# Blocked attention and a gated feed-forward layer on one core: 2 KB pieces for the stored weight blocks, wider products of zeros, and a new placement of the steps

## The chip, the cores and the metric

The kernel runs on one core of a Trainium2 chip. The metric is the device time of one execution in microseconds (us). Three executions of the kernel before took 804.26, 806.49 and 806.54 us, a median of 806.49 us. The engines are PE (TensorE; its weight loads are PEld), DVE (VectorE), ACT (ScalarE), POOL (GpSimd) and SP (SyncE, which here only issues transfers). A transfer is issued in the program order of SP or of ACT (SPq and ACTq in the trace) and moved by 16 shared DMA engines.

## The reference

```
scores = (q @ k.T) / sqrt(64)               # 8 batches, 8 heads, 576 positions, head size 64
mask   = local (the last 32 keys)  for heads 0 to 3
         strided (every 32nd key)  for heads 4 to 7
attn   = softmax(where(mask, scores, -1e9)) ; x = attn @ v     # x: 4608 tokens x 512
h = x @ w_in                                # 512 x 2048
g = h if h >= 1;  0 if h <= -1;  else (h + 1)**2 / 4
out = g @ w_out                             # 2048 x 512
```

All inputs and the output are float32.

## The kernel before, in words

The masks leave only blocks of the score matrix, so each batch is four units of attention: u0 and u1 (local heads), u2 and u3 (strided heads). One unit goes through steps that the program names by a letter: scores on PE (`s`, L592), adding the mask while leaving PSUM (`m`, L652, DVE), row maximum (`x`, L678, DVE), subtracting it (`b` on DVE or `a` on POOL, L682), exponential (`e`, L689, ACT), row sum (`q`, L693, DVE), adding a small constant (`k` on DVE or `p` on ACT), reciprocal and normalising (`w` on DVE or `r` on POOL; L705, L706), a transpose on DVE (`t`, L743), a trip through DRAM (`j`, `J`), the product with v on PE (`v` or `V`, L779), and a split of the result into a high and a low part (`h` on ACT, L841, and `l` on DVE, L850). Two steps fetch q and k (`Q`) and v (`F`).

The feed-forward part makes each float32 product of three products of 128x512 in a reduced format (high by high, high by low, low by high). Tokens come in a chunk of 512 (c = 0), two more such chunks (c = 1 and 2), and then in blocks of 1024 tokens. For c = 0 to 2 the program loops over 16 slices f of the hidden size: 12 products (L887) make `h` for the slice, ACT bends and squares it (L891, L894), and DVE closes the slice with a gate (L897, the minimum of two values). The gate also frees the PSUM bank in which `h` was summed. For c = 1 and 2 the banks are b2 and b3 in turn for f = 0 to 3 of c = 1, and then b2, b3 and b0 in turn: so the products of f = 2 and 3 wait for the gates of f = 0 and 1, and from f = 5 on each slice waits for the gate of the slice three before it. For c = 0 and the last pieces of c = 0 inside c = 1, the products with w_out (L947) run between those of w_in.

From there on the kernel uses a scheme that needs seven products instead of eight for a two by two grid of blocks, and for it sums of weight blocks. These are made on the core: step `C` or `Y` adds the blocks (L499; on POOL or on DVE), `N` or `O` combines the sums (L504; POOL or DVE), `R` rounds them (L508, ACT), `D` keeps the rest (L512, DVE). `K` stores the weight blocks in DRAM (L490, L491) and `S` the sums (L515), both issued from ACT; `fetch_w` (L971) reads single blocks back on SP, into a ring of seven buffers. The blocks of 1024 tokens then run `up_block` (L1040) and `down_block` (L1135); for the latter `G.s` splits an operand on ACT and DVE (L996, L997), `G.t` (DVE) or `G.p` (POOL) makes a sum of operands (L1096), and `G.r` takes a result out of PSUM.

The order of all this is written out in the table AGENDA: a position in the PE program (in units of six products of 128x512, negative ones inside c = 0), and the steps that are emitted there. Nothing is moved afterwards: each engine runs its instructions in that order, and waits only for the data and the buffers that it needs. The first four lines of the table hold batch 0, with the raw loads and the splitting of the first weights, and 37 products of zeros (`Z`, L577), which write into PSUM banks that hold nothing yet.

Of the kernel before, what the change touches and what calls it, by code (L numbers as in the profile page):

```python
# [1326 lines left out]
```

## Time and profile before

| | before |
|---|---|
| runs, us | 804.26, 806.49, 806.54 (median 806.49) |
| the profiled execution: its own time, us | 806.21 |
| the profiled execution: span, first to last instruction, us | 804.4 |
| mean granted TensorE clock | 0.998 of 2.4 GHz |
| PE busy in the span | 793.8 us, 99% |
| DVE, ACT and POOL busy | 620.6, 505.2 and 258.2 us |

The span is what the profiler sees between the first and the last instruction of the program; the execution's own time is 1.8 us longer. PE is busy in nearly all of it, so the table alone says little: what can be won or lost is in the few places where PE waits, and in how close the engines that feed it run behind it. A row of the timeline gives the start, the duration, the engine, the line, the operation with the tile written and the tiles read, how many such instructions are merged in the row, and in brackets the idle time of the engine before it and what ended it.

### The profile page before, as it was taken

How to read it: one execution, taken by the hardware profiler on the slowest of the kernel's cores; microseconds unless marked ns; L12 is line 12 of the kernel's file. 1: busy time of each engine (PE TensorE's matmuls, PEld its weight loads, DVE VectorE, ACT ScalarE, POOL GpSimd, SP SyncE). 2: the span in 40 equal slices, each digit the busy share in tenths (PEclk: the TensorE clock that was granted, in tenths of full speed). 3: DMA queues.
4: the chain of work that ended last, by engine and by line, in shares of the span. 5: the costliest groups of instructions: out<-in, count | busy, mean ns of one | idle time of the engine just before them, and what ended most of it. 6: DMA issues, size and time to landing. Idle time of an engine off the chain costs nothing.

```text
span 804.4 us, 17840 instructions
## 1 busy us (share of the span) xinstructions
PE 793.8 (99%) x6921; PEld 648.5 (81%) x6921; DVE 620.6 (77%) x882; ACT 505.2 (63%) x857; POOL 258.2 (32%) x202
## 2 busy tenths in 40 slices
PE   8999999999999999999999999999999999999998
PEld 6778888788888877878888888888888888888886
DVE  5899879999898999978679787575777764566673
ACT  5899764566774555677764455778554667775442
POOL 5366335796674320022141102132434001224000
PEclk9999999999999999999999999999999999999999
DMA  9948878799899899898889778777777676666765
GB/s 348 407 187 273 319 271 324 254 290 307 282 322 319 292 295 352 272 295 275 256 247 292 239 222 266 261 233 211 223 248 239 210 238 198 192 194 189 217 200 170
DMA packets 107699, 209.78 MB, mean 261 GB/s; under 512 B 17760, under 2 KB 33376, under 8 KB 105568
## 3 DMA queue, kind: packets, MB, share of 16 engines
q1 hardware_dynamic: 100560, 179.15, 69.8%
q10 hardware_dynamic: 7056, 29.49, 9.5%
q8 instruction: 55, 0.90, 0.4%
q14 instruction: 28, 0.23, 0.1%
HBM read 161.94 MB, written 46.66 MB: 259 GB/s over the span
## 4 chain that ended last, share of the span: by engine, by line
PE 91%; DVE 5%; ACT 1%; DMA 1%; issue 1%; POOL 1%; SPq 0%; POOLq 0%; DVEq 0%
PE yo L1135 22%; PE y L1040 16%; PE h L887 13%; PE zo L1135 10%; PE z L1040 8%; PE xo L1135 5%; PE o L947 4%; PE x L1040 4%; PE xp L779 3%; PE sc L592 3%; DMA qk<-in_qk_s 1%; PE tp L719 1%; DVE st L512 1%; DVE pr L682 1%; DVE st L678 0%
## 5 line engine op out<-in xcount | busy, mean ns | idle before, releaser
L1135 PE MATMUL yo<-hl,wr 128*128 128x512 f32 x768 | 177.6, 390 | 0.0
L1135 PEld LDWEIGHTS yo<-hl,wr 128*128 128x128 f32 x768 | 143.6, 188 | 30.9 <-DVE hl L997 0.9
L1040 PE MATMUL y<-x,wr 128*128 128x512 f32 x576 | 139.9, 389 | 0.0
L1040 PEld LDWEIGHTS y<-x,wr 128*128 128x128 f32 x576 | 108.0, 188 | 22.5
L887 PE MATMUL h<-xq_a,w 128*128 128x512 f32 x384 | 123.5, 395 | 1.9 <-DVE g L897 1.9
L1096 POOL TENSOR_TENSOR ga<-gb,ga 128x1024 f32<-128x1024 f32 x17 | 44.1, 2598 | 235.9 <-DVE ga L897 175.6
L997 DVE TENSOR_TENSOR hl<-ga,hl 128x1024 fp32r<-128x1024 f32 x48 | 63.5, 1338 | 37.0 <-ACT hl L996 36.9
L1135 PE MATMUL zo<-hl,wr 128*128 128x512 f32 x384 | 89.5, 391 | 0.0
L887 PEld LDWEIGHTS h<-xq_a,w 128*128 128x128 f32 x384 | 72.0, 188 | 18.6 <-DVE g L897 2.8
L1135 PEld LDWEIGHTS zo<-hl,wr 128*128 128x128 f32 x384 | 71.5, 188 | 15.9 <-DVE hl L997 0.6
L996 ACT CAST hl<-ga 128x1024 fp32r<-128x1024 f32 x48 | 50.0, 1052 | 51.1 <-PE yo L1135 16.3
L887 PE MATMUL h<-xq_b,w 128*128 128x512 f32 x192 | 73.6, 391 | 0.1
L1040 PE MATMUL z<-x,wr 128*128 128x512 f32 x288 | 73.5, 391 | 0.0
L1040 PEld LDWEIGHTS z<-x,wr 128*128 128x128 f32 x288 | 53.7, 188 | 11.4 <-DVE ga L1022 0.2
L894 ACT ACTIVATE tmp<-tmp 128x512 f32<-128x512 f32 x96 | 60.8, 634 | 3.0
L997 DVE TENSOR_TENSOR hl<-gb,hl 128x1024 fp32r<-128x1024 f32 x36 | 48.7, 1366 | 14.4 <-ACT hl L996 14.3
L996 ACT CAST hl<-gb 128x1024 fp32r<-128x1024 f32 x36 | 37.7, 1056 | 31.3 <-PE zo L1135 15.3
L504 POOL TENSOR_TENSOR st<-st 128x256 f32<-128x256 f32 x48 | 50.5, 1054 | 14.2 <-DVE st L705 6.6
L897 DVE SCALAR_TENSOR_TENSOR ga<-ga,tmp 128x512 f32<-128x512 f32 x48 | 33.0, 688 | 28.3 <-ACT tmp L894 28.0
L891 ACT ACTIVATE u<-h,half 128x512 f32<-128x512 f32 x48 | 32.8, 684 | 31.4 <-PE h L887 23.9
L469 POOL TENSOR_TENSOR raw<-raw 128x512 uint32<-128x512 uint32 (+1 forms) x34 | 35.6, 1057 | 42.3 <-DVE raw L465 16.6
L682 POOL TENSOR_TENSOR pr<-pr,st 128x384 f32<-128x384 f32 (+3 forms) x17 | 25.6, 1508 | 67.8 <-DVE st L678 67.8
(124 smaller groups left out, 1413.1 us busy)
## 6 DMA issues: line engine op xcount, KB each, us to landing
wr<-ks SPq DMA_DIRECT2D x224, 256.0 KB, 4.0
wr<-kq SPq DMA_DIRECT2D x168, 256.0 KB, 3.4
ks<-st ACTq DMA_DIRECT2D x16, 1024.0 KB, 6.8
raw<-in_w SPq DMA_DIRECT2D x30, 512.0 KB, 9.6
qk<-in_qk_s SPq DMA_DIRECT2D x16, 604.0 KB, 6.4
qk<-in_qk_l SPq DMA_DIRECT2D x16, 576.0 KB, 6.4
kq<-w ACTq DMA_DIRECT2D x16, 512.0 KB, 3.6
v<-in_v_l SPq DMA_DIRECT2D x21, 384.0 KB, 5.2
```

Source lines behind the costliest of these rows:

```text
L469: nc.gpsimd.tensor_tensor(out=raw[:, :, 1], in0=raw[:, :, 1], in1=raw[:, :, 0], op=ALU.add)
L504: eng.tensor_tensor(out=st[:, to, 1], in0=st[:, x, 1], in1=st[:, y, 1], op=op)
L682: eng.tensor_tensor(out=pr, in0=pr, in1=st[:, 0].unsqueeze(2).broadcast_to(list(pr.shape)), op=ALU.add)
L887: nc.tensor.matmul(o_ps[c, f], weight(f, 0, h)[:, x, e:e + P], xq[c][y][:, cc], start=first and n == 0, stop=last and n == len(todo) - 1)
L891: nc.scalar.activation(u, h, AF.Relu, bias=half, scale=0.5)
L894: nc.scalar.activation(u, u, AF.Square)
L897: nc.vector.scalar_tensor_tensor(out=to, in0=h, scalar=1.0, in1=u, op0=ALU.max, op1=ALU.min)
L996: nc.scalar.copy(t[:, 0], src)
L997: nc.vector.tensor_tensor(out=t[:, 1], in0=src, in1=t[:, 0].bitcast(F32), op=ALU.subtract)
L1040: nc.tensor.matmul(to, w_[:, a, c * P:(c + 1) * P], xc[m][:, b, c], start=m in (1, 2, 5) and c + q == 0, stop=c == 1 and q == 2, skip_grou ...
L1096: eng.tensor_tensor(out=to, in0=x, in1=y, op=op)
L1135: nc.tensor.matmul(to, w_[jj][:, a, d * P:(d + 1) * P], t[:, b, jj], start=m in (1, 2, 5) and k + jj + q == 0, stop=k == NP // 2 - 1 and j ...
```

## The change

Three things are changed. The tiles in DRAM that hold the weight blocks and their sums have the block as the outermost dimension, so that one block of 256 KB is contiguous; a store of sums then goes in pieces of 2 KB for each partition and block instead of 8 KB for each partition, a store of two weight blocks in pieces of 2 KB instead of 4 KB, and a read of one block takes 128 neighbouring pieces of 2 KB instead of 128 that lie 6 or 8 KB apart. The products of zeros cover the whole width of their tile (384 columns instead of 256), and there are 24 instead of 37. And all steps behind batch 0 stand at other places in the table, with some of them on another engine: of the operand sums 33 instead of 27 run on DVE and 19 instead of 25 on POOL; of the subtractions of the maximum 18 instead of 14 on DVE and 13 instead of 17 on POOL; of the normalisings 15 instead of 16 on DVE and 17 instead of 16 on POOL; one more of the sums of weight blocks (`Y`) is on DVE. The set of attention tiles that use the banks b4 and b5 is another one.

```diff
--66.69 0Zs0:17 0o0 0s0 0o1 0i0 0X0 0s1 0i1 0S0 0o3 0g1 0x1 0s2 0Zv0:3 0Zf0:3 0m2 0e0 0a1 A0.0 0s3 0i3 0e1 0x2 0q0
+-66.69 0Zs0:10 0o0 0s0 0o1 0i0 0X0 0s1 0i1 0S0 0o3 0g1 0x1 0s2 0Zv0:2 0Zf0:2 0m2 0e0 0a1 A0.0 0s3 0i3 0e1 0x2 0q0
...
-    kept = [[(dram.tile([P, 3, 2, HF], F32, tag=f"kq{i}{j}", name=f"kq_{i}_{j}"),
-              dram.tile([P, 4, 2, HF], F32, tag=f"ks{i}{j}", name=f"ks_{i}_{j}")) for j in range(NP)] for i in range(2)]
+    kept = [[(dram.tile([3, P, 2, HF], F32, tag=f"kq{i}{j}", name=f"kq_{i}_{j}"),
+              dram.tile([4, P, 2, HF], F32, tag=f"ks{i}{j}", name=f"ks_{i}_{j}")) for j in range(NP)] for i in range(2)]
...
-        nc.scalar.dma_start(kept[i][j][0][:, :2], t[:, :2])
-        nc.scalar.dma_start(kept[i][j][0][:, 2], t[:, 3])
+        nc.scalar.dma_start(kept[i][j][0][:2].rearrange("a p x e -> p a x e"), t[:, :2])
+        nc.scalar.dma_start(kept[i][j][0][2], t[:, 3])
...
-        nc.scalar.dma_start(kept[i][j][1], sums.pop((i, j)))
+        nc.scalar.dma_start(kept[i][j][1].rearrange("a p x e -> p a x e"), sums.pop((i, j)))
...
-            N = min(t.shape[1], 256)
+            N = t.shape[1]
...
-            nc.sync.dma_start(ring[n].bitcast(F32), kept[i][j][which][:, at])
+            nc.sync.dma_start(ring[n].bitcast(F32), kept[i][j][which][at])
...
-    MORE = set("2s2 2v0 2v1 3s0 3s2 3v1 4s0 4s1 4v0 5s0 5s2 5v1 5v2 6s3 7s0 7s1 7v0 7v1".split())
+    MORE = set("2s3 2v0 2v1 2v2 3s1 3s2 3v1 3v2 4s1 4v0 5s0 5s1 5s2 5v1 5v2 6v0 7s0 7v0 7v1".split())
```

In the changed kernel the lines behind the table have numbers that are 11 higher (L908 for the gate L897, and so on).

Where the steps have gone is seen in three places, all at the start of c = 1. The first is DVE around the gate of f = 0 (the tile `h_0`), while units u0 and u1 of batch 2 run beside it. Before:

```order
L897 SCALAR_TENSOR_TENSOR g_0_1979<-h_0_1840,u_0_1909 128x512
L693 TENSOR_REDUCE st_0_1905<-pr_0_1904 128x12
L701 TENSOR_SCALAR st_0_1905<-st_0_1905 128x12
L705 RECIPROCAL st_0_1905<-st_0_1905 128x12
L706 TENSOR_TENSOR pr_0_1904<-pr_0_1904,st_0_1905 128x768
L743 STREAM_TRANSPOSE t_0_0_1985<-pr_0_1904 128x6x2x32
L743 STREAM_TRANSPOSE t_0_1_1987<-pr_0_1904 128x6x2x32
L512 TENSOR_TENSOR st_1_1968<-st_1_1968 128x4x256
```

And in the changed kernel, with the same tiles under other buffer numbers:

```order
L704 TENSOR_REDUCE st_0_1890<-pr_0_1889 128x12
L712 TENSOR_SCALAR st_0_1890<-st_0_1890 128x12
L689 TENSOR_REDUCE st_1_1933<-pr_1_1932 128x6
L716 RECIPROCAL st_0_1890<-st_0_1890 128x12
L717 TENSOR_TENSOR pr_0_1889<-pr_0_1889,st_0_1890 128x768
L693 TENSOR_TENSOR pr_1_1932<-pr_1_1932,st_1_1933 128x384
L754 STREAM_TRANSPOSE t_0_0_1951<-pr_0_1889 128x6x2x32
L754 STREAM_TRANSPOSE t_0_1_1953<-pr_0_1889 128x6x2x32
L908 SCALAR_TENSOR_TENSOR g_0_1984<-h_0_1826,u_0_1895 128x512
L523 TENSOR_TENSOR st_1_1938<-st_1_1938 128x4x256
```

The gate of f = 0 has moved behind the whole of unit u0 and behind the mask, the maximum and the subtraction of unit u1; only the rest of the weight sums (L512, now L523) is still behind it.

The second place is DVE from the gate of f = 1 on. Before, the gates of f = 2 and f = 3 stand here:

```order
L678 TENSOR_REDUCE st_3_2102<-pr_3_2101 128x10
L682 TENSOR_TENSOR pr_3_2101<-pr_3_2101,st_3_2102 128x10x54
L652 TENSOR_TENSOR pr_2_2135<-sc_2_0_2073,m_str 128x6x54
L652 TENSOR_TENSOR pr_2_2135<-sc_2_1_2074,m_str 128x6x54
L897 SCALAR_TENSOR_TENSOR g_0_1979<-h_2_2021,u_2_2117 128x512
L678 TENSOR_REDUCE st_2_2136<-pr_2_2135 128x12
L693 TENSOR_REDUCE st_3_2102<-pr_3_2101 128x10
L897 SCALAR_TENSOR_TENSOR g_0_1979<-h_3_2120,u_3_2145 128x512
```

In the changed kernel, from the gate of f = 2 on (before these rows stands the gate of f = 1, and behind them the maximum of unit u3 and then the gate of f = 3):

```order
L908 SCALAR_TENSOR_TENSOR g_0_1984<-h_2_2024,u_2_2060 128x512
L663 TENSOR_TENSOR pr_2_2103<-sc_2_0_2063,m_str 128x6x54
L663 TENSOR_TENSOR pr_2_2103<-sc_2_1_2064,m_str 128x6x54
L663 TENSOR_TENSOR pr_3_2108<-sc_3_0_2037,m_str 128x4x54
L663 TENSOR_TENSOR pr_3_2108<-sc_3_1_2038,m_str 128x4x54
L663 TENSOR_TENSOR pr_3_2108<-sc_3_0_2037,m_str 64x2x54
L663 TENSOR_TENSOR pr_3_2108<-sc_3_1_2038,m_str 64x2x54
L689 TENSOR_REDUCE st_2_2104<-pr_2_2103 128x12
L693 TENSOR_TENSOR pr_2_2103<-pr_2_2103,st_2_2104 128x12x54
L510 TENSOR_TENSOR st_3_2121<-w_3_1055 128x4x256
L704 TENSOR_REDUCE st_2_2104<-pr_2_2103 128x12
L515 TENSOR_TENSOR st_3_2121<-st_3_2121 128x256 x4
```

The gate of f = 2 has moved up to stand right behind that of f = 1, and the gate of f = 3 down, behind the masks of two units, two maxima, a subtraction, a row sum, and a sum of weight blocks with its four combinations.

The third place is POOL at the same time. Before:

```order
L504 TENSOR_TENSOR st_0_1793<-st_0_1793 128x256 x4
L499 TENSOR_TENSOR st_1_1968<-w_1_914 128x4x256
L504 TENSOR_TENSOR st_1_1968<-st_1_1968 128x256 x4
L499 TENSOR_TENSOR st_2_2099<-w_2_1001 128x4x256
L632 MEMSET pr_3_2101 128x10x10
```

In the changed kernel:

```order
L515 TENSOR_TENSOR st_0_1754<-st_0_1754 128x256 x4
L510 TENSOR_TENSOR st_1_1938<-w_1_899 128x4x256
L515 TENSOR_TENSOR st_1_1938<-st_1_1938 128x256 x4
L717 TENSOR_TENSOR pr_1_1932<-pr_1_1932,st_1_1933 128x384
L643 MEMSET pr_2_2103 128x12x10
```

The normalising of unit u1 (L717), which DVE did before between the gates of f = 1 and f = 2, is now on POOL, and the transposes that wait for it stand ahead of the gate of f = 1 on DVE.

## Rows read from the trace of the kernel before

**Rows 1.** The page: busy time of PE in the span (share, instructions), and the chain of waits by engine.

```profile
PE 793.8 (99%) x6921; PEld 648.5 (81%) x6921; DVE 620.6 (77%) x882; ACT 505.2 (63%) x857; POOL 258.2 (32%) x202
...
PE 91%; DVE 5%; ACT 1%; DMA 1%; issue 1%; POOL 1%; SPq 0%; POOLq 0%; DVEq 0%
```

**Rows 2.** Stretches of the span: start and end, length, then the busy time of PE, PEld, DVE, ACT and POOL in us (instructions), the granted clock, the DMA engines' share, and GB/s. The rows are the time of the raw weight loads, c = 1 and 2, the first down block, and a late stretch of which nearly all transfers are reads of stored blocks.

```profile
20.00:40.00 20.00, 19.41 (x331) 15.22 (x325) 17.71 (x42) 17.22 (x42) 7.57 (x7) 0.91 1.03 407
...
116.00:237.00 121.00, 119.08 (x1719) 96.53 (x1718) 111.03 (x179) 75.11 (x145) 84.07 (x68) 1.00 0.89 299
...
237.00:321.00 84.00, 83.40 (x680) 67.33 (x673) 76.53 (x87) 43.52 (x65) 25.00 (x15) 1.00 0.92 312
...
700.00:720.00 20.00, 20.00 (x90) 16.57 (x89) 11.26 (x16) 15.34 (x25) 4.82 (x2) 1.00 0.63 195
```

**Rows 3.** The timeline of PE, where slices or scores begin: f = 2 of c = 1 (133.36), the scores of u3 and u2 and behind them f = 3 (136.17, 137.72), f = 5 (144.80), a product with v (147.75), f = 7 (152.88), and scores in the first down block (300.69).

```profile
133.36 0.39 PE L887 MATMUL h<-xq_a,w 128*128 128x512 f32 x1
...
136.17 1.62 PE L592 MATMUL sc<-qk 64*64 64x54 f32 x88
137.72 0.50 PE L887 MATMUL h<-xq_a,w 128*128 128x512 f32 x1
...
144.80 0.50 PE L887 MATMUL h<-xq_a,w 128*128 128x512 f32 x1 [1.34 <-DVE g L897]
...
147.75 1.60 PE L779 MATMUL xp<-pT,v 64*64 64x32 f32 x96
...
152.88 0.50 PE L887 MATMUL h<-xq_a,w 128*128 128x512 f32 x1 [0.58 <-DVE g L897]
...
300.69 0.57 PE L592 MATMUL sc<-qk 64*64 64x54 f32 x24 [0.57 <-DMA qk<-in_qk_s]
```

**Rows 4.** The chain that ended last, in order of time (start, us, what): twelve products behind a product with v, and twelve behind wide products.

```profile
62.64 2.95 PE o L947 x12
65.59 2.72 PE h L887 x12
```

**Rows 5.** The timeline of DVE from the middle of c = 1, f = 0 on. The rows L897 at 127.44, 136.34 and 144.06 are the gates of f = 0, 1 and 2.

```profile
127.44 0.68 DVE L897 SCALAR_TENSOR_TENSOR g<-h,u 128x512 f32<-128x512 f32 x1
128.44 0.95 DVE L693 TENSOR_REDUCE st<-pr 128x12 f32<-128x768 f32 x1 [0.32 <-ACT pr L689]
...
131.85 2.35 DVE L512 TENSOR_TENSOR st<-st 128x1024 fp32r<-128x1024 f32 x1
134.13 1.00 DVE L652 TENSOR_TENSOR pr<-sc,m_loc 128x128 f32<-128x128 f32 x4
...
136.34 0.69 DVE L897 SCALAR_TENSOR_TENSOR g<-h,u 128x512 f32<-128x512 f32 x1
136.94 0.54 DVE L693 TENSOR_REDUCE st<-pr 128x6 f32<-128x384 f32 x1
137.41 1.12 DVE L652 TENSOR_TENSOR pr<-sc,m_str 128x216 f32<-128x216 f32 x4
138.56 0.19 DVE L705 RECIPROCAL st<-st 128x6 f32<-128x6 f32 x1
...
139.37 0.64 DVE L743 STREAM_TRANSPOSE t<-pr 128x192 f32<-128x192 f32 x2
139.93 0.68 DVE L678 TENSOR_REDUCE st<-pr 128x10 f32<-128x540 f32 x1
140.64 2.57 DVE L682 TENSOR_TENSOR pr<-pr,st 128x540 f32<-128x540 f32 x1
143.25 0.90 DVE L652 TENSOR_TENSOR pr<-sc,m_str 128x324 f32<-128x324 f32 x2
144.06 0.68 DVE L897 SCALAR_TENSOR_TENSOR g<-h,u 128x512 f32<-128x512 f32 x1
144.66 0.82 DVE L678 TENSOR_REDUCE st<-pr 128x12 f32<-128x648 f32 x1
...
146.61 1.89 DVE L504 TENSOR_TENSOR st<-st 128x256 f32<-128x256 f32 x4
...
148.54 0.77 DVE L693 TENSOR_REDUCE st<-pr 128x12 f32<-128x648 f32 x1
...
154.28 1.20 DVE L512 TENSOR_TENSOR st<-st 128x1024 fp32r<-128x1024 f32 x1
155.40 1.75 DVE L499 TENSOR_TENSOR st<-w 128x1024 f32<-128x1024 f32 x1
```

**Rows 6.** The timeline of POOL: the one instruction that ran beside the DVE row at 140.64.

```profile
140.23 2.40 POOL L499 TENSOR_TENSOR st<-w 128x1024 f32<-128x1024 f32 x1
```

**Rows 7.** Groups of POOL instructions by line and shape (busy us, mean ns of one, idle time before): the normalising of a unit of 384 columns.

```profile
L706 POOL TENSOR_TENSOR pr<-pr,st 128x384 f32<-128x384 f32 x3 | 2.8, 943 | 4.7 <-DVE st L705 4.6
```

**Rows 8.** The timeline of all engines at the start: the first run of zeros, the copy on ACT that waits for the second fetch of q and k, and the first reduction on DVE.

```profile
0.99 3.81 PE L577 MATMUL sc<-zeros 128*128 128x256 bf16 x17 [0.99 <-DVE zeros L378]
...
5.86 0.19 ACT L435 COPY raw<-qk 1x1 f32<-1x1 f32 x1 [3.84 <-DMA qk<-in_qk_l]
...
7.54 0.56 DVE L659 TENSOR_REDUCE st<-sc 128x6 f32<-128x384 f32 x1 [6.61 <-PE sc L616]
```

**Rows 9.** The timeline of ACT and its queue: the two transfers of a store of weight blocks (L490, L491).

```profile
121.06 0.33 ACTq L490 DMA_DIRECT2D kq<-w  x1
121.43 1.22 ACTq L491 DMA_DIRECT2D kq<-w  x1
```

More of the change, by code (lines that the diff above doesn't have):

```diff
@@ new lines @@
+16.5 2t2 2j2 2J2 2e3 2q3 2p3 K02
+17.45 3s0 3s1 2r3
+17.95 3m0 3x0
+19.45 3b0
+19.95 2t3
+20.5 3m1 3x1
+21.45 S13 C15 N15 R12 R14 3e0 3q0
+22.5 D14 S14
+24.5 3b1 3e1
+25.95 2v2 2j3
+26.5 3p0
+27.45 2h2
+27.95 2l2 3q1 C16 3k1 3w0 C17 R15
+29.45 3Q2 3s3 K17 3s2 O16
+29.95 D15 S15 3w1
+30.5 K04
+31.95 R16 3t0
+32.5 3m2 3x2 3a2 3e2
+33.45 D16 N17 2F4 2J1 2J3 2V1 2h3 3q2 3p2 4Q0 2l3
+33.95 S16
+34.5 C00 D12 3j0 3t1 3j1 3r2
+35.45 3J0
+37.95 3m3 3x3
+38.5 3b3 3e3
+39.45 2h1
+39.95 R17 Y02 N02
+40.5 4s1 3t2
@@ new lines @@
+41.95 S12 3q3 3k3 3r3 4s0 4m0 4x0 K07 4a0 4e0 3t3
+42.5 R02 Y01
+43.45 4m1 4x1
+43.95 D17
+45.45 3F0
+45.95 3F1 D02 3v0 3h0
+46.5 N00 R00
+47.95 3j2 C03 4Q2
+49.45 4q0 4k0 S02 3F3
+50.5 3J2 3v2 4w0 4t0
+51.45 D00 S17
+52.5 G0s10
+53.45 3h2 O01 G0t30
+53.95 N03 R03 3j3
+55.95 4b1 Y04 D03 4e1 S03
+58.5 4s2 4m2 4x2
+59.45 3J3
+59.95 3J1 3F4 4q1 N04 3F2 3V1 3h3 3h1
+61.45 G0t32 4p1 4b2 4w1 4t1 R04 K06 D04 4j0
+61.95 G0p60
+63.45 S00
+63.95 G0t31
+64.5 Y05
+65.45 4F1
+66.5 4F0 4J0
+67.45 4j1 4F3 S04 4s3
@@ new lines @@
+109 5r0
+111 S07 G0s32
+113 4h1 G0r01 G0s33
+115 S06 G0s40 4h3 X1.-7 5t0 5j0 G0s41
+117 X1.3
+119 G0s42 5m2 G0s43
+121 5s3 X1.1 X1.-6 X1.7 X1.-5 5F0 G0r30 X1.2 5F1 X1.6
+123 G0r40 X1.5 G0r41 5x2 5a2
+124.5 G0r31
+125.5 X1.-4
+126.5 5e2 5q2 5k2 5w2 X1.4
+130.5 5J0
+131.5 5p1 5t2
+133.5 5m3 5j2
+135.5 5x3 5a3 5e3
+137.5 5q3
+138.5 5v0 5h0 5k3 6Q0 5r1 5F3 5t1 5j1
+144.5 5J1
+145.5 5J2
+146.5 G1s11 6s0 6m0
+150.5 5F2 6s1 5v2 5F4 6x0 5r3 5t3
+151.5 5h2
+153.5 6b0 6m1 6x1
+155.5 6e0 6a1 5j3
+156.5 6q0
@@ new lines @@
+158.5 G1s10 G1p60
+159.5 6e1 6q1
+160.5 6Q2
+163.5 5J3 6p0
+165.5 6w0
+166.5 6t0
+169.5 6j0
+170.5 6s2 6m2 5V1 X2.1 6J0 6x2 6a2
+172.5 6k1 6F1 G1p61
+174.5 6F0
+179.5 G1s12 G1t62 5h3
+181 G1s13
+183 G1s20 G1t40
+185 6e2 6q2 6k2 6r2 G1s21
+187 G1s22
+189 6F4 5h1 6t2 6j2 G1s23 G1r11 6s3 6m3 6x3 6v0 6h0
+193 7Q0 G1s60
+195 6w1 6t1 G1r10
+197 6J2 G1s61
+199 6b3 6j1 G1s62
+201 6e3 G1r21 6q3 G1t63 G1s63
+203 G1s70 G1p50 7s0 G1s71 G1s72 G1r60 7s1 6F3 G1r20 7m1 G1r61 G1t43 6p3
+205 G1s73 6w3 6t3
+207 G1s50 6J1 7x1 7b1
@@ new lines @@
+209 6j3 G1p51 G1s51
+213 6J3 G1t53 G1s53 G1p52 G1s52 6v2
+215 G1t41 G1s30
+217 6F2
+219 6h2 G1s31 G1r50 G1r00 G1r51 G1r01
+221 G1s32 G1s33 7e1
+223 6V1 6h3 G1t42 X2.-7 G1s40
+225 X2.-6 G1s41
+229 X2.7 G1s42
+231 X2.-5
+233 G1s43 X2.3 X2.5 G1r31 X2.6 G1r30 X2.2 X2.-4
+235 G1r40 G1r41
+238.5 7m0
+239.5 X2.4 7q1 7p1 7w1
+241.5 7Q2
+244.5 G2s10
+245.5 7x0 7F0
+256.5 7b0
+258.5 G2s11
+259.5 7e0 7q0
+267.5 G2p61
+269.5 6h1
+272.5 7k0 7w0 7t0 7j0
+273.5 7s2 7m2 7x2 7a2
+284.5 7t1 7F1 7j1
+287.5 7J0
+291.5 G2s12 7e2 7q2
@@ L257 @@
+345 X3.-6 X3.7 G2r31 X3.-5 X3.6
+347 G2r40 X3.5
+349.5 G2r41
+351.5 X3.-4 X3.4
+356.5 G3s10
+365.5 G3t60
+381.5 G3s11 G3t61
+403.5 G3s12 G3t62
 405 G3s13
 407 G3s20
[L259 to L262 removed]
+409 G3s21 G3p41
+411 G3s22 G3r10 G3p63
+413 G3s23
+415 G3p40 G3s60
 417 G3s61
[L264 to L276 removed]
```

376 lines of the change are left out of this document (124 added, 252 removed).

## The prediction, made before the changed kernel ran

> **What bounds the kernel now.** I read the page first, for who is busy: PE works 793.8 of 804.4 us, and the chain of waits is PE for 91% [rows 1]. The reader should see that nothing outside PE can give much: all of PE's idle time is 10.6 us, and part of it is the start and the drain. Then the stretches, for where the engines that feed PE have no room left: in c = 1 and 2 DVE is busy for 111.0 of 121 us, in the first down block for 76.5 of 84, while PE idles for 1.9 us and for 0.6 us in them; in the late stretch PE is full and DVE works 11.3 of 20 us [rows 2]. Then PE's own timeline, for what ended each wait: two waits in c = 1, of 1.34 and 0.58 us, end with a gate on DVE, and one of 0.57 us in the down block ends with a fetch of q and k [rows 3]. Last DVE's timeline before the larger of these: the gate of f = 2 starts only at 144.06, because the subtraction at 140.64 takes 2.57 us [rows 5]. A POOL instruction that started at 140.23 and took 2.40 us ends at 142.63 [rows 6], and DVE is done 0.58 us later: DVE was held up by it.
>
> So the price of this change is decided by how far DVE runs behind PE up to about 321 us. Later a new order has nothing to remove; it could only add.
>
> **The change, part by part.** The sum is made against the profiled execution's 806.21 us; the median of the runs is 806.49, 0.28 more, and I add that at the end.
>
> *Zeros.* The first run of 17 took 3.81 us [rows 8], 224 ns for 256 columns, 0.875 ns a column. Ten of 384 columns take 3.36 us, so the first scores can begin 0.45 us earlier. But their second half needs the second fetch, for which ACT's copy waited until 5.86, and DVE's first reduction, which waits for these products, came at 7.54 [rows 8]. The gain is between 0 and 0.45; I take 0.2, the middle, since the fetch covers part of it. The other zeros have 5,376 columns in place of 5,120 and stand in gaps: nothing.
>
> *Changes between attention and wide products.* Counted in the order, PE comes back from narrow products to wide ones 42 times instead of 41. Twelve wide products take 2.95 us behind a product with v and 2.72 behind wide ones [rows 4]: one more costs 0.2.
>
> *The gates at the start of c = 1.* Three gates move, and each can be worked out from the times of the kernel before. Gate of f = 0: ahead of it now stands all that DVE did before up to the gate of f = 1, less the rest of the weight sums (131.85 to 134.13, 2.28 us) and less the gate of f = 0 itself with the wait behind it (127.44 to 128.44, 1.00 us). That gate ended at 136.34 + 0.69 = 137.03, so the gate of f = 0 now ends at 137.03 - 2.28 - 1.00 = 133.75 [rows 5]. PE wanted to begin f = 2 at 133.36 [rows 3]: 0.4 us lost, where 5.2 us were to spare.
>
> Gate of f = 1: behind 133.75 come the rest of the weight sums (1.20 to 2.35 us), a row sum (0.54), two small steps (0.19 each, the second measured, the first taken like it), the transposes (0.64) and the gate (0.68) [rows 5]; before the transposes now stands POOL's normalising, 0.94 us [rows 7], which is a new wait: queued behind the transposes on DVE are the gates of f = 1 and f = 2, and PE waits for those. The end is at 138.1 to 139.3. PE would be ready for f = 3 at 133.8 + 2.81 + 1.55 (from 133.36 to 136.17 and on to 137.72) = 138.2 [rows 3]. Lost: 0 to 1.1, and I take 0.5.
>
> Gate of f = 2: it follows at once, some 4 us earlier than before, so the 1.34 us go. What is late next is the gate of f = 3. From the gate of f = 2 at about 139.3 it has ahead of it masks (0.90 and 1.12), a maximum (0.82), a subtraction (taken like that maximum, 0.82), a sum of weight blocks (1.75), a row sum (0.77), four combinations (1.89) and a maximum (0.68) [rows 5], together 8.75, and ends at 148.7. PE reaches f = 6 at 138.7 + 3 times 2.72 + 1.6 for the product with v + 0.2 [rows 3, 4] = 148.7. Level; with the next hold-up of DVE it is late, and I take 0.2.
>
> *The other 28 slices of c = 1 and 2.* Before, one gate cost PE 0.58 us. Now the gates come with margins of a few tenths at the start, and the same kinds of hold-up (2.57 for a subtraction, 2.35 for what can take 1.20 us [rows 5]) fall on them. At best nothing is lost, at worst three hold-ups of 1 us; I take 1.0.
>
> Gates together: 0.4 + 0.5 + 0.2 + 1.0 - 1.34 - 0.58 = +0.2, between -1.5 and +3.2.
>
> *Operand sums.* Six more run on DVE instead of POOL. They lie in the down blocks, where DVE has 7.5 us to spare in the first [rows 2] and more later; what hides them is PE's own work, and if that cover is gone, an operand comes late by about one sum. I count 0.
>
> *The wait at 300.69.* In the order, the scores of u2 of batch 5 still come 36 wide products behind those of u1, which free the buffer for the fetch. The 0.57 us stay.
>
> *The stores and reads.* The sums (16 of 1 MB) go in 2 KB pieces instead of 8, two thirds of the stored blocks (16 of 0.5 MB) in 2 KB instead of 4. With raw loads of long pieces the DMA engines moved 407 GB/s at a share of 1.03, with reads in 2 KB pieces 195 GB/s at 0.63 [rows 2]: 395 against 310 when full. The 25 MB then cost 25.2 MB x (1/310 - 1/395) = 17 us of all 16 engines. The trace has no contiguous block read, so the gain of the reads is bounded from both sides: none, or all of that difference for 392 reads of 256 KB, 71 us. Engines with a share of 0.89 and 0.92 [rows 2] hide the cost just so; PE waits for no read of a block. I take 0, between -0.6 (the fetch of rows 3 lands in time) and +3.
>
> The Trainium skill bears on this ("DMA: Bandwidth & Descriptors", Why small descriptors are slow): it gives about 3 cycles of overhead for each packet beside one cycle for 32 bytes, which is 268 cycles instead of 259 for 8 KB, an estimate of 3.5%; by that the finer stores would cost 2 us of the engines instead of 17, and nothing in time. The rows of pieces of 2 KB speak for the larger price, though other things than the size may lie in them.
>
> Sum: -0.2 + 0.2 + 0.2 + 0 = +0.2, so 806.4 for the profiled execution and 806.7 for the median.
>
> **The rivals.** *A, the new order fits.* The gates come without lateness and the finer reads let the fetch land early: 1.92 + 0.57 + 0.45 go, and 806.49 - 2.9 = 803.6. For it: all four are waits that the trace shows, and POOL, which held up DVE, has six operand sums and four subtractions fewer. Against it: the gate of f = 0 is late by the times of the kernel before already.
>
> *B, DVE's lateness becomes PE's.* Slower. The gates of f = 0, 1 and 3 of c = 1, and two or three behind them, stand with no margin; the place is c = 1 and 2. Each hold-up of 1 to 1.8 us (2.35 - 1.20, or 2.57 - 0.8) then reaches PE: 0.4 + 1.1 + 1.0 and three more of 1.2 are 6.1 us, less the 1.92 that go: 806.49 + 4.2 = 810.7. It decides as soon as these gates are late by more than 0.7 us each on average. For it: DVE has only 10 us of idle time in 121. Against: PE's own delay gives each following gate more room.
>
> *C, the finer stores.* Slower too: the second transfer of a store held ACT's queue for 1.22 us against 0.33 for the first [rows 9]; if a store of four times the pieces does that, ACT bends the next slice 0.9 us later, in 16 stores over c = 1 and 2, and reads queue behind 17 us more of transfers. With a third of the 16 uncovered that is 5 us: 811.
>
> [...]
>
> *D, the change does nothing in time*: the zeros have 9,216 columns instead of 9,472 and the FLOPs are the same, so every move could be covered. That is the forecast's number as well.
>
> **How the numbers follow.** Forecast and D 0.52, A 0.22, B 0.15, C 0.11. What this kernel's runs can tell from no change is about 0.3%, or 2.4 us. The forecast's own range is 804.5 to 809.2; it gives 0.44 to the same, 0.03 to faster, 0.05 to slower. A gives 0.18 to faster and 0.04 to the same; B and C together 0.23 to slower and 0.03 to the same. Together: faster 0.21, same 0.51, slower 0.28. The range reaches to most of A and B: 803.0 to 811.0.
>
> **What would show it.** In the changed profile: PE's waits for gates in c = 1 sit at f = 2, 3 and 6 with some tenths each, and none at f = 5; DVE's first reduction comes 0.2 us earlier; the wait for q and k near 300 us stays; the DMA share of c = 1 and 2 rises above 0.89; nothing changes behind 330 us. I am wrong if PE idles in c = 1 and 2 for under 0.7 us or over 4, if a wait for a stored block appears on PE, or if ACT's issues of sums take more than 0.5 us.

## The result, and the profile after

The changed kernel took 811.81, 813.45, 817.24 and 819.18 us, a median of 815.35; four runs of the kernel before beside them had a median of 806.51. The ratio is 1.0118, with a 95% interval of 1.0093 to 1.0144: the change made the kernel 1.2% slower, where the prediction had no change (806.7) and at most 811.0. The six runs taken later gave 814.68 (ratio 1.0111, 1.0075 to 1.0147). The runs of the changed kernel lie 7 to 10 us apart, those of the kernel before mostly within 4.

The profiled execution is the fastest of the four: 811.81 us, span 810.0. The first lines of its page, and the chain of waits, which answer to [rows 1], and the two queues of transfers (packets, MB, share of 16 engines):

```profile
PE 794.1 (98%) x6908; PEld 646.3 (80%) x6908; DVE 625.1 (77%) x891; ACT 504.4 (62%) x858; POOL 227.1 (28%) x192
...
q1 hardware_dynamic: 100560, 179.15, 70.2%
q10 hardware_dynamic: 15248, 29.49, 9.9%
...
PE 73%; DVE 11%; DMA 10%; ACT 2%; issue 2%; POOL 1%; SPq 0%; ACTq 0%; POOLq 0%; DVEq 0%
```

PE is busy for as long as before (794.1 against 793.8 us). The 5.6 us that the span has grown are nearly all idle time of PE, and in the chain DMA has risen from 1% to 10%. So the place to search is where PE waits for transfers. PE's waits between 125 and 330 us (us in total, times, longest):

```profile
PE xp L790 <- DMA pT<-there: 3.8, 2, 3.3
PE zo L1146 <- DMA wr<-ks: 2.1, 1, 2.1
PE h L898 <- DVE g L908: 1.3, 2, 0.7
PE xo L1146 <- DMA wr<-kq: 0.6, 1, 0.6
```

Before, this view had two lines, 1.9 us for gates and 0.6 for q and k [rows 3]. The gates cost less now. New are waits for attention's trip through DRAM and for stored blocks. Stretches cut at the program's own marks (first and last product of c = 0 with w_out, first product of the first down block, first product of the up block behind it), with the columns of [rows 2], for the kernel before:

```profile
35.36:133.52 98.16, 97.62 (x906) 78.68 (x905) 88.54 (x165) 78.58 (x150) 51.90 (x49) 1.00 0.76 278
133.52:237.27 103.75, 101.79 (x1473) 82.75 (x1472) 95.76 (x155) 66.56 (x126) 71.42 (x57) 1.00 0.88 294
237.27:320.91 83.64, 83.07 (x665) 67.12 (x665) 76.22 (x86) 43.16 (x64) 24.73 (x15) 1.00 0.92 311
```

and for the changed kernel:

```profile
34.40:131.81 97.41, 97.32 (x861) 78.04 (x858) 89.96 (x169) 77.91 (x152) 46.43 (x44) 1.00 0.72 252
131.81:240.78 108.97, 103.86 (x1472) 84.53 (x1471) 93.30 (x157) 63.96 (x123) 63.49 (x58) 0.98 0.92 308
240.78:327.08 86.30, 83.55 (x707) 67.91 (x705) 79.26 (x92) 46.33 (x69) 15.12 (x9) 1.00 0.94 306
```

The stage of c = 1 and 2 is 5.2 us longer, the first down block 2.7; start and c = 0 together are 1.7 shorter, and all that follows is 0.6 shorter. In this execution the loss lies in two stages. The largest wait, on PE's timeline:

```profile
177.18 0.90 PE L790 MATMUL xp<-pT,v 64*64 64x32 f32 x48
181.35 0.33 PE L790 MATMUL xp<-pT,v 54*64 54x64 f32 x4 [3.27 <-DMA pT<-there]
182.18 1.33 PE L790 MATMUL xp<-pT,v 54*64 54x64 f32 x36 [0.49 <-DMA pT<-there]
183.44 0.79 PE L898 MATMUL h<-xq_a,w 128*128 128x512 f32 x1
```

and the granted clock there (the column before the DMA share), which falls to its lower level behind the wait:

```profile
178.20:181.40 3.20, 0.05 (x2) 0.08 (x3) 2.73 (x3) 0.95 (x2) 3.12 (x3) 1.00 0.92 285
181.40:183.40 2.00, 1.50 (x40) 1.32 (x40) 0.00 (x0) 0.03 (x1) 1.67 (x3) 0.67 0.92 226
183.40:184.40 1.00, 1.00 (x5) 0.83 (x3) 0.40 (x2) 1.00 (x10) 0.00 (x0) 0.50 1.07 369
184.40:185.40 1.00, 1.00 (x4) 0.75 (x3) 0.99 (x5) 0.97 (x6) 0.00 (x0) 0.50 0.90 341
```

So 3.8 us of waiting (3.27 and 0.49) are followed by a stretch at the lower of the two clock levels (0.50, 1.2 GHz). By an estimate it costs some 1.9 us more: the 40 small products from 181.35 on took 1.66 us where 48 take 0.93 elsewhere in the trace (163.44), and five of 512 columns behind them 2.20 where twelve take 2.72 [rows 4]. The product that waits is `2V1` (batch 2, units 1 and 3); it needs what the steps `2J1` and `2J3` bring back from DRAM, four transfers each (called gathers here). Before, `2J1` stood at position 15.95, `2J3` at 29.45 and `2V1` at 33.45; the new table has `2F4 2J1 2J3 2V1` in a row at 33.45. SP's queue:

```profile
164.45 0.33 SPq L549 DMA_DIRECT2D v<-in_v_s  x1
164.87 15.16 SPq L775 DMA_DIRECT2D pT<-there  x8
180.13 0.85 SPq L536 DMA_DIRECT2D qk<-in_qk_l  x2
```

The eight gathers (L775) took SP 15 us to issue. Within these, by the view of SP's waits from 157 to 183 us, it stood for other transfers (the second row is a wait ahead of them):

```profile
SPq L775 <- DMA ks<-st: 3.7, 1, 3.7
SPq L549 <- PE xp L790: 3.5, 1, 3.5
SPq L775 <- DMA qk<-in_qk_s: 3.3, 1, 3.3
SPq L775 <- DMA kq<-w: 3.0, 3, 2.0
SPq L775 <- DMA v<-in_v_s: 1.9, 1, 1.9
```

A gather (L775) reads neither a stored block nor q or v. The instruction list of the changed program as built, SP's transfers with the semaphores that each waits for, says why it waits for them:

```
L549 DMA v_3_0_2657<-in_v_s 128x640 [waits DMAHW7_49,PE_49]
L775 DMA pT_1_2659<-there_1_2154 32x4x96 [waits DMAHW3_49,DMAHW2_49]
L775 DMA pT_1_2659<-there_1_2154 32x4x96 [waits DMAHW5_49]
L775 DMA pT_1_2659<-there_1_2154 32x4x96 [waits DMAHW7_49]
L775 DMA pT_1_2659<-there_1_2154 32x4x96 [waits DMAHW0_49]
L775 DMA pT_3_2664<-there_3_2488 32x4x160 [waits DMAHW6_49,DMAHW1_49]
```

Each transfer signals its end on one of eight semaphores, DMAHW0 to 7, taken in turn by SP's and ACT's transfers together, and waits until the transfer that had this one before has landed. So a transfer isn't issued before the one eight places ahead of it, on either queue, is done, and a late store holds what is issued behind it whether it is read or not. The eight semaphores belong to this program as it was built; no run here shows a program with more of them.

The wait of 2.13 us at 312.88 is of another kind. Timeline of DVE, and then of SP's queue, around the sums of results (L1129) which a put (L945) sends out:

```profile
301.40 1.21 DVE L523 TENSOR_TENSOR st<-st 128x1024 fp32r<-128x1024 f32 x1
302.54 1.21 DVE L1107 TENSOR_TENSOR g<-g 128x1024 f32<-128x1024 f32 x1
303.78 0.69 DVE L1129 TENSOR_TENSOR kept<-yo,kept 128x512 f32<-128x512 f32 x1
```

```profile
293.44 6.89 SPq L982 DMA_DIRECT2D wr<-ks  x6
304.50 0.34 SPq L945 DMA_DIRECT2D out<-kept  x1
304.95 1.16 SPq L982 DMA_DIRECT2D wr<-ks  x1
```

The new table has `D07 G0t42` directly ahead of the results (`G0r50` and the like), where the old one had `D07` further in front. The put waited 4.1 us for DVE, by the view of SP's waits from 293 to 312 us,

```profile
SPq L945 <- DVE kept L1129: 4.1, 1, 4.1
```

and the read that PE waited for, the only one of `ks` that SP issued between 301 and 312 us (304.95), stood behind it. The put isn't the whole delay: the reads issued from 303 to 312 us landed after 6.2 to 8.7 us, where the page's median is 3.4.

### The profile page after: what moved, and what is told of

Same layout as the page of the kernel before. It is cut to its first block, busy times and chain, and to the rows that moved or that the text cites. A ratio compares the mean times of both kernels' runs of the same rounds, so it can differ in the third digit from the quotient of the medians.

```text
span 810.0 us, 17794 instructions
## 1 busy us (share of the span) xinstructions
PE 794.1 (98%) x6908; PEld 646.3 (80%) x6908; DVE 625.1 (77%) x891; ACT 504.4 (62%) x858; POOL 227.1 (28%) x192
## 4 chain that ended last, share of the span: by engine, by line
PE 73%; DVE 11%; DMA 10%; ACT 2%; issue 2%; POOL 1%; SPq 0%; ACTq 0%; POOLq 0%; DVEq 0%
PE yo L1146 19%; PE y L1051 16%; PE zo L1146 8%; PE h L898 8%; PE z L1051 8%; DMA raw<-in_w 5%; PE x L1051 4%; PE xo L1146 4%; PE xp L790 2%; PE o L958 2%; DVE hl L1008 2%; PE sc L603 1%; DMA there<-t 1%; DVE st L523 1%; DMA wr<-ks 1%
## 5 line engine op out<-in xcount | busy, mean ns | idle before, releaser
L1107 POOL TENSOR_TENSOR ga<-gb,ga 128x1024 f32<-128x1024 f32 x17 | 40.8, 2400 | 277.7 <-DVE ga L908 231.5
L1008 DVE TENSOR_TENSOR hl<-ga,hl 128x1024 fp32r<-128x1024 f32 x48 | 67.5, 1415 | 36.4 <-ACT hl L1007 36.4
L515 POOL TENSOR_TENSOR st<-st 128x256 f32<-128x256 f32 x48 | 44.6, 929 | 39.6 <-DVE st L510 32.5
L908 DVE SCALAR_TENSOR_TENSOR ga<-ga,tmp 128x512 f32<-128x512 f32 x48 | 32.8, 685 | 25.3 <-ACT tmp L905 25.2
L1146 PE MATMUL xo<-hl,wr 128*128 128x512 f32 x192 | 45.1, 391 | 0.6 <-DMA wr<-kq 0.6
```

What stands on the lines that cost most here:

```text
L515: eng.tensor_tensor(out=st[:, to, 1], in0=st[:, x, 1], in1=st[:, y, 1], op=op)
L908: nc.vector.scalar_tensor_tensor(out=to, in0=h, scalar=1.0, in1=u, op0=ALU.max, op1=ALU.min)
L1008: nc.vector.tensor_tensor(out=t[:, 1], in0=src, in1=t[:, 0].bitcast(F32), op=ALU.subtract)
L1107: eng.tensor_tensor(out=to, in0=x, in1=y, op=op)
L1146: nc.tensor.matmul(to, w_[jj][:, a, d * P:(d + 1) * P], t[:, b, jj], start=m in (1, 2, 5) and k + jj + q == 0, stop=k == NP // 2 - 1 and j ...
```

## Experiments

Theory: the loss is the order of the steps in these two places. Rivals: the pieces of 2 KB (stores that take longer), and the amount of stores in this stretch, since the new table has 9 stores of weight blocks in c = 0 where the old one had 13, and so four more (3.1 MB) behind it.

**The layout undone.** The tiles in DRAM, the stores (pieces of 4 and 8 KB for each partition; the expectation's 16 is a slip) and the reads as before the change, all else as changed:

```diff
-    kept = ... dram.tile([3, P, 2, HF] ... dram.tile([4, P, 2, HF]
+    kept = ... dram.tile([P, 3, 2, HF] ... dram.tile([P, 4, 2, HF]
-            nc.sync.dma_start(ring[n].bitcast(F32), kept[i][j][which][at])
+            nc.sync.dma_start(ring[n].bitcast(F32), kept[i][j][which][:, at])
```

> The changed kernel with the blocks in DRAM laid out as before (runs of 4 and 16 KB per partition); the new order and the wider zeros stay. Theory 'order' (the loss comes from where the new order puts two sets of transfers on SP's queue): the products of batch 2 on units 1 and 3 still wait 3 to 4 us for the transposed probabilities near 178 us, and the time stays within 2 us of the changed kernel (813 to 817 us). Rival 'layout' (stores in 2 KB pieces fill the transfer engines, and everything else that moves lands late): that wait falls under 1 us, the stored blocks land after 3.5 us instead of 6.7, and the time falls by 5 us or more, to 808 us or less.

Measured: 817.87 us, ratio 1.0139 (1.0111 to 1.0167), not faster. PE still waits for the gathers:

```profile
185.11 0.48 PE L790 MATMUL xp<-pT,v 54*64 54x64 f32 x4 [3.13 <-DMA pT<-there]
```

The layout isn't the cause of this wait. That the time is 0.9 us above what the theory allowed isn't more than the scatter of these runs (814.85 to 821.77). The stores of weight blocks land late in either layout: the page gives 5.9 us from issue to landing here (first transfer of a store, median), 6.7 for the changed kernel and 3.6 for the one before.

**The zeros alone, on the kernel before.**

```diff
-            N = min(t.shape[1], 256)
+            N = t.shape[1]
-... 0Zs0:17 ... 0Zv0:3 0Zf0:3 ... 0Zf0:9 ... 0Zf0:5
+... 0Zs0:10 ... 0Zv0:2 0Zf0:2 ... 0Zf0:6 ... 0Zf0:4
```

(The counts make 24 products of 384 columns in place of 37 of 256; the expectation miscounts them.)

> The kernel before with only the products of zeros changed: 24 of up to 512 columns in place of 34 of 256. The prediction's term was -0.2 us (0 to -0.45). Rival, from the trace of the changed kernel, in which the first product of the MLP starts at 23.72 us instead of 25.16 and the granted clock doesn't fall to 0.50 between 20 and 24 us: -1.4 to -1.8 us, 804.7 to 805.1 us, with no stretch at 0.50 before 25 us.

Measured: 806.56, ratio 1.0004 (0.9991 to 1.0018): nothing. The rival fails: the earlier start of the changed profile isn't a gain of the zeros that lasts. In the run with the layout alone (below), which has the old zeros, the first product with w_out comes at 34.30 us, where the kernel before had 35.36 and the changed one 34.40: the start varies with the execution.

**One step moved**: `2J1` back in front.

```diff
-22.5 D14 S14
+22.5 D14 2J1 S14
-33.45 D16 N17 2F4 2J1 2J3 2V1 ...
+33.45 D16 N17 2F4 2J3 2V1 ...
```

> The changed kernel with one step moved: the four transfers that bring batch 2's probabilities of unit 1 back from DRAM are issued ahead of those steps of unit 3, instead of directly ahead of unit 3's four and of the products that read both. Theory 'order': the wait of 3.8 us at 178 us and the stretch of half clock behind it (about 1.5 us) go, and the time falls by 4 to 6 us, to 809 to 811.5 us. Rival 'layout' or 'full transfer engines': the same transfers are late wherever they are issued, PE still waits 2 us or more for them, and the time falls by less than 1.5 us.

Measured: 810.20 (804.79 to 814.21), ratio 1.0046 (1.0024 to 1.0069): 4.5 to 5.1 us less than the changed kernel (814.68 and 815.35), as the theory had it, and with an interval clear of the changed kernel's. The same product now runs without a wait, and four gathers take SP 3.5 us:

```profile
176.02 1.51 PE L790 MATMUL xp<-pT,v 64*64 64x32 f32 x88
```

```profile
163.71 3.52 SPq L775 DMA_DIRECT2D pT<-there  x4
```

Its profiled execution (805.46) was the second fastest of twelve, 4.7 below its median, so stages are not compared by it alone.

**The results first.**

```diff
-107 ... N07 R07 D07 G0t42 G0r50 G0r00 4V1 S01 G0t40 5p0 G0r51
+107 ... N07 R07 G0r50 G0r00 G0r51 G0r01 D07 G0t42 4V1 S01 G0t40 5p0
-113 4h1 G0r01 G0s33
+113 4h1 G0s33
```

> The changed kernel with one place of the order changed: the four sums of results (m=5, m=0) of the first super-chunk stand together ahead of the last step of a stored block's sums and of the sum of gates on VectorE, as before the change, so that the put of a result doesn't hold SP's queue for 4.1 us with the loads of blocks behind it. Theory 'order': the wait of 2.1 us for a stored block at 311 us goes, -1.5 to -2.5 us. Rival 'layout': the loads are late because blocks land late, the wait stays above 1.5 us, and the time within 0.5 us of the changed kernel.

Measured: 813.93, ratio 1.0088 (1.0061 to 1.0115), some 1 us less, which alone decides nothing, since the intervals overlap. In the profile the wait of 2.13 us is gone; one of 0.99 for another block stands a little further on, and one of 2.71 far behind:

```profile
317.85 2.35 PE L1146 MATMUL yo<-hl,wr 128*128 128x512 f32 x9 [0.99 <-DMA wr<-kq]
446.04 5.05 PE L1146 MATMUL yo<-hl,wr 128*128 128x512 f32 x21 [2.71 <-DMA wr<-ks]
```

**The layout alone, on the kernel before** (the first diff the other way round, and the two stores).

> The kernel before with only the layout of the stored blocks changed (pieces of 2 KB); old order, old zeros. The prediction's term was 0 (-0.6 to +3). Theory 'order' (the run of the changed kernel in the old layout was 2.5 us slower than the changed kernel, inside the scatter of both): 804 to 807 us. Rival 'layout costs' (stores land later, queue behind them): 809 us or more.

Measured: 805.79, ratio 1.0001 (0.9986 to 1.0017). The layout costs and gives nothing in time. The reads do gain: a block lands 3.4 and 3.2 us after its issue (`wr<-ks` and `wr<-kq`, medians of the page) instead of 4.0 and 3.4. And the first transfer of a store of weight blocks lands after 4.1 us, so the 6.7 of the changed kernel come mostly from the order.

**The changed kernel once more.**

> The changed kernel itself once more, without an edit, since its four runs lie 7.4 us apart (811.81 to 819.18) and those of the kernel before 2.6. Theory 'order': in the slower runs the wait at 178 us, the stretch at half clock behind it and the late blocks behind 240 us are there with other lengths, so the median stays at 813 to 817 us. Rival 'one disturbed profile': the median falls under 812 us.

Measured: 814.68 (810.45 to 820.57), ratio 1.0111 (1.0075 to 1.0147). Its profiled execution was the slowest, 820.57, and shows part of what makes the scatter. Timelines of DVE and of ACT, and PE's clock behind the gathers:

```profile
157.46 3.21 DVE L693 TENSOR_TENSOR pr<-pr,st 128x768 f32<-128x768 f32 x1
```

```profile
155.47 0.69 ACT L902 ACTIVATE u<-h,half 128x512 f32<-128x512 f32 x1 [2.73 <-DMA kq<-w]
```

```profile
190.00:192.00 2.00, 2.00 (x6) 1.52 (x6) 2.00 (x6) 1.43 (x6) 0.00 (x0) 0.50 0.84 318
```

The subtraction that took 1.07 us in the faster execution (156.16) took 3.21 here, beside a sum of weight blocks on POOL of 2.42 us (157.45). In the faster one such a sum ran beside it too (156.37), but began 0.2 us behind the subtraction, and there it was POOL's that took longer (3.12). PE waited 2.90 us for a gate at 163.95 in this execution, 0.56 in the other. The clock stood at 0.50 from some 186.5 to 193.4 us, where the faster execution had it so from 182.1 to 185.5. ACT, whose queue stood at a store until one of the eight semaphores was free, bent the next slice 2.73 us late, but it did so by 2.50 in the faster execution (154.16) as well; that is not the difference. The stage of c = 1 and 2 is 4.5 us longer than in the faster execution; the other 4.3 us lie in the other stages and were not traced.

**Both places at once.**

> The changed kernel with both edits at once: unit 1's transfers back from DRAM issued earlier, and the sums of results ahead of the other VectorE work. If the two are independent, the gains seen add up (-5.1 and -1.4): 808.5 to 809 us, with no PE wait near 178 us and none over 1 us near 306 us. Rival 'the waits move' (a queue that runs ahead meets the next late block): the time stays at 810 us or above and PE waits as long for other blocks.

Measured: 808.21 (804.41 to 814.56), ratio 1.0031 (1.0010 to 1.0053). Together they give 6.5 to 7.1 us of the 8.8 to 9.2 that the change had lost (815.35 against 806.51, and 814.68 against the 805.53 measured beside it). The forecast that the two effects add up held, but what the second place adds (810.20 to 808.21) lies within the intervals: its wait is shown, its price in time isn't. The wait for the stored block has shrunk to 0.19:

```profile
308.62 2.33 PE L1146 MATMUL zo<-hl,wr 128*128 128x512 f32 x9 [0.19 <-DMA wr<-ks]
```

**Both, and four stores early** (`K01`, `K02`, `K04`, `K14`; `K01` stood behind c = 0 before the change as well, so the number agrees with the old table, not each store):

```diff
-1.955 K14  ... 11.95 ... K01 ... 16.5 ... K02 ... 30.5 K04
+-55.035 K01 ... -45.5 ... K02 ... -28.5 K04 ... -20.5 K14
```

> The kernel with both places mended, and besides four stores of weight blocks (blocks 1, 2 and 4 of the first matrix, block 4 of the second, 3.1 MB) issued before the first super-chunk ends, at the latest where the order before had issued a like number, instead of between 137 and 175 us. Theory 'crowded window' (the new order took 3.1 MB of stores out of the stretches 40 to 60 and 80 to 100 us, where the transfer engines are 0.40 busy, into 100 to 320 us, where they are 0.93 busy against 0.89 before): the share of 100 to 320 us falls to about 0.89, the waits for blocks shrink, and the time falls by 1.5 to 4 us against the kernel with the two places mended, with less scatter. Rival 'order alone': within 1 us of that kernel; or slower, where a store holds ScalarE's queue in the busy stretch before 100 us.

Measured: 808.21 (805.15 to 809.99), ratio 1.0026 (1.0009 to 1.0043). No gain, though the scatter is half as wide. Stage by stage, from PE's timeline of one execution each (us):

| kernel | c = 0 | c = 1 and 2 | first down block | rest |
|---|---|---|---|---|
| before | 98.2 | 103.8 | 83.6 | 479.9 |
| changed | 97.4 | 109.0 | 86.3 | 479.3 |
| changed, slowest execution | 99.0 | 113.5 | 87.6 | 480.2 |
| one step moved, second fastest execution | 97.2 | 103.1 | 86.1 | 479.3 |
| both places | 97.7 | 106.0 | 85.5 | 479.4 |
| both, four stores early | 100.4 | 103.5 | 84.6 | 479.1 |
| stores early alone | 99.5 | 106.2 | 86.8 | 482.3 |
| both, stores elsewhere early | 101.4 | 102.8 | 84.1 | 479.4 |
| new until 130, then before | 103.2 | 103.4 | 83.3 | 479.3 |
| the same, stores spread behind | 97.7 | 107.7 | 86.4 | 479.4 |

In these executions what the stores gave back in the second and third column they took in the first. But the second column differs by 4.5 us between two executions of the changed kernel, and the kernel with one step moved took 103.1 there with all four stores in it. So the table suggests a price of the stores of some 2.5 us and doesn't prove it; the equal medians show that moving them wins nothing.

**Only the stores early**, at -41.5, -33.5, -23.8 and -20.5; the two places as changed.

> The changed kernel with only the four stores of weight blocks issued earlier (block 1 and 2 of the first matrix near 60 and 75 us, block 4 of each near 100 us); the transfers back from DRAM and the sums of results stay where the change put them. Theory 'queue of eight' (each transfer waits for the end of the one eight issues before it, SP's and ScalarE's counted together, so that slow stores in front hold the eight transfers of units 1 and 3): with the stores of 3.0 us gone from in front of them the wait near 178 us shrinks from 3.8 to 1 to 2.5 us, and ScalarE no longer waits 3.0 us for a store at 174 us; 810.5 to 813 us. Rival 'position alone' (eight transfers right ahead of their product are late whatever stands in front): the wait stays at 3 us or above; 813.5 to 816 us.

Measured: 814.11, ratio 1.0114 (1.0096 to 1.0132). The wait has shrunk to what the first theory said, with nothing done to the gathers themselves:

```profile
181.47 0.80 PE L788 MATMUL xp<-pT,v 54*64 54x64 f32 x36 [1.77 <-DMA pT<-there]
```

So how late the gathers are depends on which stores stand ahead of them. The time didn't fall as the theory had it: in the profiled execution c = 0 took 2 us more (99.5), and what lies behind the first down block 3 us more (482.3), with a wait of 2.34 us for a stored block at 443.77. A wait of this kind came in the slowest execution of the changed kernel too (0.89, at 449.83) and in the run with the results first (2.71). The clock fell behind a wait of 1.81 us for a block in this execution,

```profile
309.00:311.10 2.10, 0.29 (x3) 0.01 (x1) 2.10 (x4) 1.64 (x2) 0.00 (x0) 1.00 1.02 361
311.10:313.10 2.00, 2.00 (x8) 1.65 (x9) 2.00 (x2) 0.00 (x0) 0.20 (x1) 0.88 1.03 373
313.10:315.10 2.00, 2.00 (x6) 1.56 (x5) 0.13 (x1) 1.01 (x1) 0.00 (x0) 0.50 0.99 357
```

and didn't behind one of 2.13 in the profile of the changed kernel:

```profile
312.90:314.90 2.00, 2.00 (x9) 1.59 (x9) 1.79 (x2) 0.00 (x0) 0.00 (x0) 1.00 1.02 353
```

**All three edits**, the stores as in the last run.

> The changed kernel with the three edits: unit 1's transfers earlier, the sums of results first, and the four stores earlier, now at places further from the stretch near 50 us where the earlier try made PE wait 1.16 us for a split of weights. Theory 'order': without those waits (1.16 and 0.94 us) 805.5 to 807.5 us, no PE wait over 1 us from 130 us on. Rival 'nothing left there': 808 us, as with the two places alone.

Measured: 808.01 (804.59 to 813.53), ratio 1.0041 (1.0016 to 1.0065): the rival's number. From 130 us on PE waits 0.6 us at most, as the theory had it, but 1.54 at 128, and 0.54 and 0.44 us earlier in c = 0.

**The new order up to 130 us, the old one behind it.** The five stores that the new c = 0 had put off stand at -23.8, -9.5, -6.2, -3.8 and -0.5; zeros and layout as changed.

> The new order up to the end of chunk 0 (130 us), with the five stores that the new order had put off issued there, and the order before from then on; zeros and layout as changed. Theory 'order' (the loss of the change lies wholly between 132 and 321 us; the new order of chunk 0 took 97.4 us from the first output product to the last against 98.2): 805 to 806 us, same as before or up to 1 us faster. Rival 'the new order of chunk 0 lost through what it put off': with the stores put back ScalarE is held in 100 to 130 us, 807 us or above.

Measured: 811.61, ratio 1.0079 (1.0056 to 1.0102). In the profiled execution, the fastest of six (808.84), the old order takes its old times behind 130 us (103.4 and 83.3). So the loss of the change comes from what stands behind 130 us, its order or the stores that were put there; this run moved both. But c = 0 costs 103.2. ACT, and PE behind it:

```profile
120.73 0.69 ACT L892 ACTIVATE u<-h,half 128x512 f32<-128x512 f32 x1 [7.05 <-DMA kq<-w]
```

```profile
123.39 1.75 PE L888 MATMUL h<-xq_a,w 128*128 128x512 f32 x4 [3.96 <-ACT xq_a L842]
```

Three stores of two transfers each were issued in those 7 us, each waiting for its semaphore by the instruction list, and ACT bends nothing in the meantime.

**Four of these stores spread behind c = 0**, one by one, at 2.51, 17.45, 35.95 and 51.45.

> The kernel of the new order until 130 us once more, with four of its five stores taken out of the crowd at 112 to 124 us (where ScalarE waited 7.05 us for stores, and PE 3.96 us for ScalarE) and placed one by one behind it, near 139, 154, 171 and 187 us. Theory 'spacing' (a store costs when it stands close behind others on ScalarE's queue, not by itself): chunk 0 takes 97.4 to 98.5 us again instead of 103.2, the rest as in the kernel before, 802.5 to 805.5 us in all. Rival 'amount' (four more stores behind 130 us cost there what they cost before it): chunks 1 and 2 take 2 us or more longer than 103.4, 806 us or above.

Measured: 811.57, ratio 1.0076 (1.0051 to 1.0101). The stage of c = 0 is back at 97.7, but c = 1 and 2 take 107.7 and the down block 86.4, with the old order in both: the theory 'spacing' fails, and the times are those of the rival 'amount'. The rival's cause isn't shown. Most of the 4.3 us by which c = 1 and 2 are longer than in the run before this one is a late gate behind a long DVE instruction, and the clock behind that (the third row is a stretch):

```profile
190.78 2.65 DVE L513 TENSOR_TENSOR st<-st 128x1024 fp32r<-128x1024 f32 x1 [1.97 <-ACT st L509]
194.21 0.50 PE L888 MATMUL h<-xq_a,w 128*128 128x512 f32 x1 [1.91 <-DVE g L898]
195.20:196.20 1.00, 1.00 (x4) 0.70 (x4) 1.00 (x4) 0.00 (x0) 0.92 (x2) 0.50 0.00 0
```

The same kind of instruction took DVE 1.22 us at 194.07; at 190.78 a sum on POOL (189.95, 2.39 us) ran beside it. Whether a store that held ACT brought the two together wasn't tried. No version here beats the kernel before.

## Why the prediction was wrong, step by step

- *The stores and reads*: this is the step that failed. It asked only for sizes and bandwidth, took 0 (-0.6 to +3), and said "PE waits for no read of a block"; attention's trip through DRAM had no term in the sum at all. The trip cost 3.8 us of waiting and about 1.9 of halved clock; reads of blocks cost 2.7, less the 0.57 for q and k that went: 7.8 us in place of 0. With -0.6 for the gates and -1.7 for start and c = 0 these are 5.5 of the 5.6 us by which the span grew. Missing was the place on SP's queue: the steps `2J1`, `G0r00` and the `K` had moved past other transfers, as the order showed, and I followed only the gates on DVE.
- *The gates at the start of c = 1, and the other 28 slices*: the mechanism was right in the main, the size too high. Gates cost 1.28 us now, 0.72 at f = 3 (0.5 forecast) and 0.56 at f = 10, none at f = 2, 5 and 6; the two of before are gone. The term was +0.2 and measured 1.28 - 1.92 = -0.6. At f = 3 the forecast was near partly by luck. The new wait for POOL is there, but behind it DVE stood for a transfer too, which the working didn't have, and by these rows the gate would have been in time without the second wait:

```profile
134.59 0.38 DVE L754 STREAM_TRANSPOSE t<-pr 128x192 f32<-128x192 f32 x1 [1.01 <-POOL pr L717]
135.89 0.38 DVE L754 STREAM_TRANSPOSE t<-pr 128x192 f32<-128x192 f32 x1 [0.92 <-DMA there<-t]
```

  That a sum on POOL beside it lengthens DVE's work, which the forecast counted on, came true in the slowest execution (3.21 us for 1.07).
- *Zeros*: -0.2 forecast; DVE's first reduction came at 7.40 instead of 7.54 [rows 8], and with the zeros alone the time didn't change.
- *Rival C, finer stores*: wrong in both its parts. ACT's issue of a sum of 512 pieces took 0.37 us instead of 0.33, and the queue of stores 9.9% of the 16 engines instead of 9.5%, some 4 us (0.099 x 810.0 - 0.095 x 804.4) instead of the 17 that I had worked out from [rows 2]. The rule of the Trainium skill ("DMA: Bandwidth & Descriptors", Why small descriptors are slow), by which it was an estimated 2 us, was nearer. The layout alone came out at 1.0001.
- *Rival B, lateness becomes PE's*: right in the place (c = 1 and 2); its 810.7 is near the fastest run (811.81) and half of what the medians lost. In the fastest execution the cause is another: not DVE's lateness, but that of transfers. In the slowest the wait of 2.90 us for a gate is B's.
- *Rival A, the new order fits*: the waits that it counted on did go (1.92 for gates, 0.57 for q and k); others came in their place.
- Two of the signs that were to show me wrong came: PE idles 5.0 us in c = 1 and 2, and waits for stored blocks. The wait for q and k near 300 us, which was to stay, went. The DMA share of c = 1 and 2 did rise, from 0.88 to 0.92; with the four stores early (the run with all three edits) it is 0.88 again.

Settled by runs: 6.5 to 7.1 of the loss are two places on SP's queue, 4.5 to 5.1 of it the gathers by themselves, and the layout and the zeros are nothing. The remaining 2.5 us (1.0031) are not settled: that they are the four stores, which would cost about as much before 130 us as behind it, is argued from single executions. With both places mended PE still waited 2.8 us for gates from c = 1 to the start of the first down block, where the kernel before waited 1.9. Why the old c = 0 carries 13 stores in 98.2 us, where the new one with 13 or 14 took 99.5 to 103.2, wasn't tried.

## What to carry to other kernels

When a step moves, write down for each transfer that it issues what stands in front on its queue and what stands behind it, and how far ahead of its reader it is; the eight transfers that were put directly ahead of their product cost more than all gates together. A wait of an issuing engine for another engine's result (a put behind a sum, 4.1 us here) holds every load behind it on that queue. And a transfer may wait for stores that it has nothing to do with, where the program's transfers share semaphores, so a count of transfers in flight belongs in the sum beside the bytes. Before a difference of 2 us between stages is explained, two executions of one kernel should be compared.
